# Turning a kernel's intermediate outputs by DMA transposes on ScalarE's queue, with a new order of the first loads

## The chip, the cores and the metric

The kernel runs on one core of one Trainium2 chip. The metric is the device time of one execution in microseconds; several executions are run and their median is given. A profile of one further execution shows what each engine did.

The engines are named as in the profile: PE is TensorE (matmuls; its weight loads are PEld), DVE is VectorE, ACT is ScalarE, POOL is GpSimd, SP is SyncE, which here only issues loads. ACTq and SPq are the instruction queues of ACT and SP, which issue transfers.

## The reference

```python
def _attn_ref(q, k, v, alpha):                     # each (4, 8, 768, 48), float32
    B, H, S, D = q.shape
    state = np.zeros((B, H, D, D), dtype=np.float32)
    y = np.zeros_like(q)
    for t in range(S):
        state = alpha[:, :, t, :, None] * state + np.einsum('bhd,bhe->bhde', k[:, :, t], v[:, :, t])
        y[:, :, t] = np.einsum('bhd,bhde->bhe', q[:, :, t], state)
    return y

def _moe_ref(x, w1, w2, w3, w_out):                # x (3072, 384), w1..w3 (384, 768), w_out (768, 384)
    h = np.maximum(np.maximum(x @ w1, x @ w2), x @ w3)
    return h @ w_out
```

The output y of the gated recurrence, heads side by side, is the input x of the feed-forward part. alpha lies between 0.8 and 1.0.

## The kernel before

**Tiling.** Time is cut into six chunks of 128 steps. A unit is one chunk of one batch with all eight heads: 24 units, u = 0 to 23, four per chunk. Two units are a group, n = 0 to 11. Group n's inputs q, k, v and alpha are loaded together (384 KB each, in rows of 192 bytes) into one of five sets of buffers (`ld[x][n % 5]`).

**A unit.** `decay` takes the logarithm of alpha for a group (L482, ACT) and its totals (L495, PE). `prep(u)` sums the logarithms along time by a matmul with a triangular matrix (L523), takes two exponentials (L526, L528, ACT), multiplies them onto q and k (L535, POOL or DVE as the table `EARLY` says), scales v (L546 on POOL, or L541 on ACT), turns q and k on PE (L556) and copies them out (L560, DVE), forms the scores (L568, PE) and masks them (L574, DVE). `output(u)` multiplies the masked scores with v (L594) and, after the first chunk, q with the carried state Z (L591); ACT scales the result into the fp16 tile `xb` (L602); PE turns `xb` in three 128 x 128 squares (L609, the step `turn`), and DVE copies the turned squares into `xT` (L613). `state(u)` carries the state on (L627 PE, L633 DVE, L640 POOL, or DVE in the first chunk).

**The feed-forward stage**, `ffn(n)`, works on a group's 256 tokens. The maximum of three products is taken as x w1 + max(0, x (w2 - w1), x (w3 - w1)), so `wd` holds the two differences, made by the four `subs` (L430, DVE), and w1 is multiplied with w_out beforehand (`turned`, L447 and L453; `folded`, L464 and L471). A stage is 36 matmuls with wd (L665), six ReLU on ACT (L675) and maxima on DVE (L680), 18 matmuls with w1o and wo (L696), two copies on ACT (L706) and two stores issued from ACT's queue (L707).

**Order.** Nothing is scheduled at run time: each engine executes its instructions in the order of the program. `Plan` collects all steps with an engine, a planned cost and a rank; `order` simulates the engines, the PSUM banks, the transfers and the clock of PE with these figures, lets every engine take the step that can start first (the lower rank where several can), and emits the instructions in the order of the planned start times. Ranks: unit u has rank u, stage n starts at 2n + `LEAD`. The order of the loads on SP is the list `FIRST` for groups 0 to 3 and the weights, and then group by group. The weights are loaded in pieces of columns, cut at `WCUTS` (rows for w_out), cast on ACT where needed (L422), and w1's and w_out's fp32 copies share one buffer.

Of the kernel before, what the change touches and what calls it, by code (L numbers as in the profile page):

```python
# [10 lines left out]
FP32 = mybir.dt.float32  # L11
# [16 lines left out]
DMA_OUT = {"SP": 0.9, "POOL": 0.9}  # L28
DMA_BOTH = {"SP": 0.2, "POOL": 0.85}
SPARE = 1.5  # L30
LEAD = 7.0
EARLY = {0: ("DVE", "POOL", "POOL"), 1: ("POOL", "DVE", "POOL"), 2: ("POOL", "DVE", "POOL"),
         3: ("POOL", "DVE", "ACT"), 4: ("POOL", "DVE", "POOL"), 5: ("POOL", "DVE", "POOL"),
         6: ("DVE", "DVE", "POOL"), 8: ("POOL", "POOL", "ACT")}
WEIGHTS = ()
WCUTS = (0, 256, 768)
SUBS = {(1, 0): "DVE", (1, 1): "DVE", (2, 0): "DVE", (2, 1): "DVE"}
FIRST = (("a", 0, 1, 2), ("k", 1, 0, 1), ("aq", 0, 0, 1), ("qk", 0, 1, 2), ("k", 0, 0, 1),
# [5 lines left out]
CLOCK_WINDOW, CLOCK_PHASE, CLOCK_WAKE, CLOCK_KEEP = 3.413, 0.0, 0.75, 0.37  # L44


# [65 lines left out]
class Plan:  # L112
# [10 lines left out]
        self.behind, self.tail = {}, {}  # L123

    def step(self, eng, cost, rank, run, reads=(), writes=(), banks=(), load=0.0, line=None,
             mode=0, late=0.0):
        i = len(self.steps)
        deps = set()
        if line is not None:
            if line in self.tail:  # L130
                self.behind[i] = self.tail[line]
            self.tail[line] = i
        for k in reads:
            if k in self.writer:
                deps.add(self.writer[k])
        for k in writes:
            if k in self.writer:
                deps.add(self.writer[k])
            deps.update(self.readers.get(k, ()))
        for k in reads:  # L140
            self.readers.setdefault(k, []).append(i)
        for k in writes:
            self.writer[k] = i
            self.readers[k] = []
        deps.discard(i)
        for k in set(reads) | set(writes):
            if k in self.users:
                self.users[k].append(i)
        for k in banks:
            self.users[k] = [i]  # L150
        self.steps.append((eng, cost, rank, run, deps, tuple(banks), load, mode, late))

    def homes(self, bank_free, keys):
        left, when, at = dict(bank_free), 0.0, {}
# [13 lines left out]
    def order(self):  # L168
# [41 lines left out]
        while len(seq) < n:  # L210
            best = None
            for e, cand in pending.items():
                pick = None
                for i in cand:
                    at = self.homes(bank_free, self.steps[i][5])
                    if at is None:
                        continue
                    t = max(ready[i], free[e], at[0])
                    turn = TURN_RANK if e == "PE" and self.steps[i][7] != mode else 0.0
                    key = (t, self.steps[i][2] + turn, i)  # L220
                    if pick is None or key < pick:
                        pick = key
                if pick is not None and (best is None or pick < best[0]):
                    best = (pick, e)
            landing = dma.next()
            if landing and (best is None or landing[0] <= best[0][0]):
                end, i = dma.next(commit=True)
                self.landed[i] = end
                finish(i, end)
                continue  # L230
            (t, _, i), e = best
            _, cost, _, _, _, banks, load, m, late = self.steps[i]
            pending[e].discard(i)
            for k, b in self.homes(bank_free, banks)[1].items():
                place[k] = b
                for j in range(self.width.get(k, 1)):
                    del bank_free[b + j]
            if e == "PE":
                if m != mode:
                    mode = m  # L240
                    cost += TURN_COST
                cost = clock.run(t, cost)
            free[e] = t + cost
            seq.append((t, i))
            if load:
                dma.add(e, t + cost + DMA_IN[e], load, i, late)
            else:
                finish(i, t + cost + HOP[e])
            if i in follows:
                arrive(follows[i], t)  # L250
        self.times = {i: t for t, i in seq}
# [4 lines left out]
def kernel(  # L256
# [69 lines left out]
    v16s = homes(7, [P, H, D], FP16, "v")  # L326
    qkTs = homes(3, [P, 2, NP, P], FP16, "qkT")
    LAs = homes(3, [P, 2, NP, P], FP16, "LA")
    xbs = homes(3, [P, DM], FP16, "xb")
    xTs = homes(NX, [P, NFT, TG], FP16, "xT")  # L330
    hTs = homes(3, [P, NJ, TG], FP16, "hT")
    obs = homes(4, [P, DM], FP32, "ob")
# [18 lines left out]
        for t in zz:  # L351
            nc.vector.memset(t, 0.0)

    plan = Plan({x: range(NBANKS) for x in ("Lp", "hp", "tp", "A", "yp", "xp", "pp", "gp", "op", "wt", "wp")})
    place = {}

    psall = pspool.tile([P, NBANKS, 512], FP32, name="psum")
# [20 lines left out]
    def load(n, lo, hi, names="aqkv"):  # L378
        cb, g = divmod(n, B // UB)
        for x in names:  # L380
            t = ld[x][n % 5]

            def run(x=x, t=t):
                nc.sync.dma_start(  # L384
                    t[:, lo:hi],
                    views[x][cb * P:(cb + 1) * P, g * HG + lo:g * HG + hi])

            plan.step("SP", 0.5, -1.0, run, line="loads",
                      writes=[(x, n % 5, h) for h in range(lo // H, hi // H)],
                      load=(1.84 if n < 3 else 1.96) * (hi - lo) / HG,  # L390
                      late=0.0 if n < 3 else SPARE)

    nparts = len(WCUTS) - 1
# [18 lines left out]
    def wload(g, part):  # L412
# [1 line left out]
                  lambda: nc.sync.dma_start(  # L414
                      piece(wst[g], g, part),
                      piece(matrices[g].rearrange("(t p) f -> p t f", p=P), g, part)),
                  writes=[("ws", g % 3, part)], line="loads",
                  load=3.1 * (WCUTS[part + 1] - WCUTS[part]) / DF)
        if g in (0, 3):
            n = NFT * (WCUTS[part + 1] - WCUTS[part])  # L420
            plan.step("ACT", 0.2 + 0.00083 * n, -0.5,
                      lambda: nc.scalar.copy(out=piece((w1h, 0, 0, wo16)[g], g, part),  # L422
                                             in_=piece(wst[g], g, part)),
                      reads=[("ws", g % 3, part)], writes=[("w", g, part)])

    def subs(g, part):
        cols = slice(WCUTS[part], WCUTS[part + 1])
        n, eng = NFT * (cols.stop - cols.start), SUBS[g, part]
        plan.step(eng, 0.2 + n * (0.0023 if eng == "POOL" else 0.00106), 0.0 if g == 1 else 3.0,
                  lambda: (nc.gpsimd if eng == "POOL" else nc.vector).tensor_sub(  # L430
                      wd[:, :, g - 1, cols], wst[g][:, :, cols], w1h[:, :, cols]),
                  reads=[("ws", g, part), ("w", 0, part)], writes=[("wd", g, part)])
# [79 lines left out]
    def prep(u):  # L512
# [47 lines left out]
        plan.step("DVE", 0.69, u, lambda: nc.vector.tensor_copy(out=qkT, in_=live[tk]),  # L560
                  reads=[tk], writes=[("qkT", u % 3)])

        def scores():
            live[Ak] = banks2(Ak, FP32)
            for j in range(NP):
                for p in range(2):
# [1 line left out]
                    nc.tensor.matmul(live[Ak][:, p, j * P:(j + 1) * P],  # L568
                                     qkT[rows, 1, j, :], qkT[rows, 0, j, :], start=True, stop=True)

        plan.step("PE", 0.23, u, scores, banks=[Ak], mode=1,
                  reads=[("qkT", u % 3), ("qkT room", u % 3)], writes=[Ak, ("LA room", u % 3)])
        plan.step("DVE", 1.3, u,
                  lambda: nc.vector.tensor_mul(  # L574
                      LA.rearrange("p a b t -> p (a b) t"),
                      live[Ak].rearrange("p a (b t) -> p (a b) t", t=P),
                      maskA.unsqueeze(1).broadcast_to([P, H, P])),
                  reads=[Ak], writes=[("LA", u % 3)])

    def output(u):  # L580
        n, i = divmod(u, UB)
        cb, b = divmod(u, B)
        qkT, LA, v16, xb = qkTs[u % 3], LAs[u % 3], v16s[u % 7], xbs[u % 3]
        Z = Zs[cb % 2][b]
        yk, xk = ("yp", u), ("xp", u)

        def outs():
            yp = live[yk] = bank(yk, [P, H, D], FP32)
            for j in range(NP):
# [3 lines left out]
                for p in range(2):  # L593
# [4 lines left out]
                  reads=[("qkT", u % 3), ("LA", u % 3), ("v16", u % 7), ("qkT room", u % 3),  # L598
                         ("LA room", u % 3)]
                  + ([("Z", cb % 2, b)] if cb else []))  # L600
        plan.step("ACT", 0.58, u,
                  lambda: nc.scalar.activation(out=xb, in_=live[yk].rearrange("p a b -> p (a b)"),  # L602
                                               func=AFT.Copy, scale=ysc),
                  reads=[yk], writes=[("xb", u % 3)])

        def turn():
            live[xk] = bank(xk, [P, NFT, P], FP16)
            for ft in range(NFT):
                nc.tensor.transpose(live[xk][:, ft, :], xb[:, ft * P:(ft + 1) * P], ident)  # L609

        plan.step("PE", 0.17, u, turn, banks=[xk], reads=[("xb", u % 3)], writes=[xk])
        plan.step("DVE", 0.35, u,
                  lambda: nc.vector.tensor_copy(out=xTs[n % NX][:, :, i * P:(i + 1) * P], in_=live[xk]),  # L613
                  reads=[xk], writes=[("xT", n % NX, i)])

    def state(u):
        n, i = divmod(u, UB)
# [102 lines left out]
    for n in range(NG):  # L720
# [5 lines left out]
                state(u)  # L726
        for u in range(n * UB, (n + 1) * UB):
            prep(u)
            for g, after, x in WEIGHTS:
                if after == u:  # L730
                    weights(g, ("v16", u % 7) if x == "v" else ("qk", u % 7, "qk".index(x)))
            output(u)
        for key in SUBS:
            if not made[key] and ("w", 0, 0) in plan.writer and ("ws", *key) in plan.writer:
                made[key] = True
# [40 lines left out]
```

## Time and profile before

| | before |
|---|---|
| median of 3 runs (us) | 159.06 (157.92 to 159.46) |
| profiled execution (us) | 158.94 |
| its span, first to last instruction (us) | 157.2 |
| PE busy (us, share of the span) | 137.1 (87%) |
| DVE / ACT / POOL busy (us) | 102.3 / 86.3 / 68.6 |
| read from HBM / written (MB) | 23.69 / 4.72 |
| L609 PE / L613 DVE (turns of xb) | 72 instructions / 24 instructions |

Times are in microseconds. A group of instructions is a line of the kernel with an engine and an operation; behind its busy time and the mean of one in nanoseconds stands the idle time of the engine just before these instructions, with what ended it. Several matmuls can be in flight at once, so that the records of single ones overlap. In the chain of work that ended last, each piece of time belongs to one engine only. A loading transfer shows twice: its issue on SPq, which is long when the queue is full, and its landing.

### The profile page before, as it was taken

What the parts mean: (1) busy time and instruction counts of PE and PEld (TensorE: products, weight loads), DVE (VectorE), ACT (ScalarE), POOL (GpSimd) and SP (SyncE); (2) the same over time, 40 slices, a digit from 0 to 9 for tenths busy, and PEclk for the clock granted to TensorE, in tenths of its full rate; (3) what the DMA queues carried; (4) which work ended last, traced back from release to release, by engine and by line L of the source; (5) the groups of instructions that cost most, each with busy time, mean ns of one, the idle gap of its engine ahead of it and who ended that gap; (6) DMA issues with size and microseconds to landing.
All of it is one profiled execution on the core that took longest, in us unless ns stands there. A gap on an engine that the chain in (4) does not pass through costs nothing.

```text
span 157.2 us, 4036 instructions
## 1 busy us (share of the span) xinstructions
PE 137.1 (87%) x1612; PEld 105.2 (67%) x1612; DVE 102.3 (65%) x172; ACT 86.3 (55%) x172; POOL 68.6 (44%) x98
## 2 busy tenths in 40 slices
PE   0264479599999999999899998999999999999990
PEld 0142357467687796888678777688797787868650
DVE  7058573588985997979759987357698494224020
ACT  3607476877176775785548546369356335424321
POOL 0051242005206285979969886279939500000000
PEclk9999999999999999999999999999999999999999
DMA  5999999989999999999999999999920110202112
GB/s 118 217 281 237 352 205 356 305 181 225 208 216 233 221 220 201 269 205 216 190 207 275 173 255 223 233 261 197 230 76 0 54 50 0 104 8 92 50 50 100
DMA packets 106226, 28.66 MB, mean 182 GB/s; under 512 B 99936, under 2 KB 105056, under 8 KB 106208
## 3 DMA queue, kind: packets, MB, share of 16 engines
q1 hardware_dynamic: 102464, 23.60, 71.9%
q10 hardware_dynamic: 3744, 4.82, 8.6%
q8 instruction: 12, 0.20, 0.5%
q14 instruction: 6, 0.05, 0.1%
HBM read 23.69 MB, written 4.72 MB: 181 GB/s over the span
## 4 chain that ended last, share of the span: by engine, by line
PE 58%; SPq 28%; DMA 7%; issue 2%; ACT 2%; POOL 1%; ACTq 0%
PE psum L665 23%; SPq L384 23%; PE psum L696 17%; DMA an<-in_alpha_dram 7%; SPq L414 5%; PE psum L556 4%; PE psum L568 3%; PE psum L523 2%; PE psum L609 2%; PE psum L594 2%; PE psum L591 2%; PE psum L627 2%; PE psum L495 1%; POOL qk L535 1%; ACT ob L706 1%
## 5 line engine op out<-in xcount | busy, mean ns | idle before, releaser
L665 PE MATMUL psum<-xT,wd 128*128 128x256 f16 x432 | 55.4, 276 | 1.7 <-DVE wd L430 1.6
L665 PEld LDWEIGHTS <-wd 128*128 128x128 f16 x432 | 40.8, 99 | 8.6 <-DVE wd L430 2.1
L680 DVE TENSOR_TENSOR hT<-psum,hT 128x512 f16<-128x512 f32 x36 | 24.4, 688 | 18.2 <-PE psum L665 14.4
L535 POOL TENSOR_TENSOR qk<-qn,ep 128x384 f16<-128x384 f32 x22 | 22.3, 1017 | 30.2 <-ACT ep L526 20.1
L574 DVE TENSOR_TENSOR LA<-psum,c 128x1024 f16<-128x1024 f32 x24 | 28.8, 1218 | 2.8 <-PE psum L568 2.7
L675 ACT ACTIVATE hT<-psum 128x512 f16<-128x512 f32 x36 | 21.3, 598 | 15.7 <-PE psum L665 14.9
L696 PE MATMUL psum<-wo,hT 128*128 128x384 f16 x144 | 27.3, 326 | 0.0
L706 ACT COPY ob<-psum 128x384 f32<-128x384 f32 x24 | 11.5, 480 | 19.7 <-PE psum L696 18.6
L546 POOL TENSOR_SCALAR v<-vn,c 128x384 f16<-128x384 f32 x22 | 13.5, 618 | 18.4 <-DMA vn<-in_v_dram 18.3
L556 PE MATMUL psum<-c,qk 128*128 128x128 f16 x192 | 16.5, 231 | 4.5 <-POOL qk L535 4.4
L696 PEld LDWEIGHTS <-hT 128*128 128x128 f16 x144 | 14.1, 98 | 9.3
L535 POOL TENSOR_TENSOR qk<-kn,en 128x384 f16<-128x384 f32 x18 | 18.0, 1000 | 2.6 <-DMA kn<-in_k_dram 1.5
L560 DVE COPY qkT<-psum 128x1024 f16<-128x1024 f16 x24 | 16.3, 687 | 3.7 <-PE psum L556 3.4
L640 POOL TENSOR_TENSOR Z<-U,G 48x192 f16<-48x192 f32 x32 | 15.7, 503 | 5.6 <-DVE U L633 4.5
L556 PEld LDWEIGHTS <-qk 128*128 128x128 f16 x192 | 12.5, 102 | 6.5 <-POOL qk L535 5.8
L482 ACT ACTIVATE la<-an 128x768 f16<-128x768 f32 (+1 forms) x15 | 10.7, 714 | 11.0 <-DMA an<-in_alpha_dram 11.0
L602 ACT ACTIVATE xb<-psum,c 128x384 f16<-128x384 f32 x24 | 13.9, 579 | 3.4 <-PE psum L594 1.9
L696 PE MATMUL psum<-w1o,xT 128*128 128x384 f16 x72 | 15.6, 326 | 0.0
L526 ACT ACTIVATE ep<-psum 128x384 f32<-128x384 f32 x24 | 11.8, 491 | 5.5 <-PE psum L523 2.5
L613 DVE COPY xT<-psum 128x384 f16<-128x384 f16 x24 | 8.5, 355 | 8.2 <-PE psum L609 7.9
L523 PE MATMUL psum<-la,c 128*128 128x384 f16 x24 | 8.5, 353 | 6.1 <-ACT la L482 6.0
L594 PE MATMUL psum<-v,LA 128*128 128x48 f16 x192 | 11.4, 187 | 0.9 <-POOL v L546 0.8
(38 smaller groups left out, 148.2 us busy)
## 6 DMA issues: line engine op xcount, KB each, us to landing
out_dram<-ob ACTq DMA_DIRECT2D x24, 192.0 KB, 2.9
an<-in_alpha_dram SPq DMA_DIRECT2D x9, 384.0 KB, 5.9
qn<-in_q_dram SPq DMA_DIRECT2D x9, 384.0 KB, 6.4
kn<-in_k_dram SPq DMA_DIRECT2D x9, 384.0 KB, 6.1
vn<-in_v_dram SPq DMA_DIRECT2D x9, 384.0 KB, 6.2
ws<-in_moe_w_dram SPq DMA_DIRECT2D x3, 768.0 KB, 6.6
an<-in_alpha_dram SPq DMA_DIRECT2D x6, 192.0 KB, 4.1
kn<-in_k_dram SPq DMA_DIRECT2D x6, 192.0 KB, 4.4
```

What stands on the lines that cost most here:

```text
L384: nc.sync.dma_start(t[:, lo:hi], views[x][cb * P:(cb + 1) * P, g * HG + lo:g * HG + hi])
L535: nc.gpsimd if eng == "POOL" else nc.vector).tensor_mul(
L556: nc.tensor.transpose(live[tk][:, w, j, :], qk[:, w, 2 * j:2 * j + 2, :], ident)
L560: plan.step("DVE", 0.69, u, lambda: nc.vector.tensor_copy(out=qkT, in_=live[tk]), reads=[tk], writes=[("qkT", u % 3)])
L574: lambda: nc.vector.tensor_mul(LA.rearrange("p a b t -> p (a b) t"), live[Ak].rearrange("p a (b t) -> p (a b) t", t=P), maskA.unsqueeze(1) ...
L594: nc.tensor.matmul(yp[:, 2 * j + p, :], LA[:, p, j, :], v16[:, 2 * j + p, :], start=(cb == 0), stop=True, skip_group_check=True)
L602: lambda: nc.scalar.activation(out=xb, in_=live[yk].rearrange("p a b -> p (a b)"), func=AFT.Copy, scale=ysc),
L640: eng.tensor_mul(Zn[rows, :, cols], U[rows, :, cols], G[rows, i * NP:(i + 1) * NP].unsqueeze(2).broadcast_to([D, NP, D]))
L665: nc.tensor.matmul(live[gk][:, jj, :], wd[:, kt, g, c0:c0 + P], xT[:, kt, :], start=(kt == 0), stop=(kt == NFT - 1))
L675: lambda h=h, gk=gk: nc.scalar.activation(out=h, in_=live[gk], func=AFT.Relu),
L680: lambda h=h, gk=gk: nc.vector.tensor_max(h, live[gk], h),
L696: nc.tensor.matmul(live[ok], a[:, i * P:(i + 1) * P], w, start=(kt == 0), stop=(kt == nk - 1))
```

## The change

- **Turns.** From unit 8 on (`CROSS = 8`), `output` no longer has the steps `turn` (PE) and the copy to `xT` (DVE). Its new step `across` on ACT scales the result into `xb` and then issues a transposing transfer from ACT's queue that writes `xb` turned into `xT`. The plan counts 0.93 us for it, with another 3.5 (`TURNED`) until `xT` can be read. `xb` has five buffers instead of three. The planned cost of a load of group 4 and later rises by `PAUSE`, 0.3 us.
- **Order of the loads.** `FIRST` begins with q, alpha, k and v of group 0, and then has pieces of w2, w1 and w3, then group 1 and w_out between them. The weights are cut in three pieces instead of two (`WCUTS`), which gives twelve loads instead of eight and six subtractions instead of four. w_out's loads now wait for all the casts of w1, whose buffer they use.
- **Engines.** Five of the six subtractions are on POOL, and `EARLY` gives other engines to products and scalings of the first ten units.
- **Dummy matmuls.** `warm(1, 0, 60)` adds 60 matmuls of zeros (128 x 256, result unused) behind unit 1's product of q, at rank 90, so where the plan has nothing else for PE.
- **Figures of the plan.** `LEAD` is 5 instead of 7, and some planned costs are other ones. `PAIRS = 99` leaves the order of the scores as it was.

```diff
-LEAD = 7.0
-EARLY = {0: ("DVE", "POOL", "POOL"), 1: ("POOL", "DVE", "POOL"), 2: ("POOL", "DVE", "POOL"),
-         3: ("POOL", "DVE", "ACT"), 4: ("POOL", "DVE", "POOL"), 5: ("POOL", "DVE", "POOL"),
-         6: ("DVE", "DVE", "POOL"), 8: ("POOL", "POOL", "ACT")}
+LEAD = 5.0
+EARLY = {0: ("DVE", "DVE", "ACT"), 2: ("POOL", "DVE", "ACT"), 3: ("POOL", "POOL", "ACT"),
+         4: ("POOL", "POOL", "ACT"), 5: ("DVE", "POOL", "POOL"), 6: ("POOL", "POOL", "POOL"),
+         7: ("DVE", "DVE", "ACT"), 8: ("POOL", "POOL", "POOL"), 9: ("POOL", "DVE", "POOL")}
-WCUTS = (0, 256, 768)
-SUBS = {(1, 0): "DVE", (1, 1): "DVE", (2, 0): "DVE", (2, 1): "DVE"}
-FIRST = (("a", 0, 1, 2), ("k", 1, 0, 1), ("aq", 0, 0, 1), ("qk", 0, 1, 2), ("k", 0, 0, 1),
-         ("w", 1, 0), ("w", 0, 0), ("a", 1, 0, 1), ("q", 1, 0, 1), ("v", 1, 0, 1), ("w", 0, 1),
-         ("w", 1, 1), ("v", 0, 1, 2), ("v", 0, 0, 1), ("k", 1, 1, 2), ("a", 1, 1, 2),
-         ("q", 1, 1, 2), ("w", 3, 1), ("w", 2, 0), ("w", 3, 0), ("v", 1, 1, 2), ("w", 2, 1),
-         ("aqkv", 2, 0, 2), ("q", 3, 0, 1), ("a", 3, 0, 1), ("k", 3, 0, 1), ("a", 3, 1, 2),
+WCUTS = (0, 256, 512, 768)
+SUBS = {(1, 0): "POOL", (1, 1): "POOL", (1, 2): "POOL", (2, 0): "POOL", (2, 1): "DVE",
+        (2, 2): "POOL"}
+FIRST = (("q", 0, 0, 1), ("a", 0, 0, 1), ("q", 0, 1, 2), ("a", 0, 1, 2), ("k", 0, 0, 1),
+         ("v", 0, 0, 1), ("w", 1, 1), ("kv", 0, 1, 2), ("w", 1, 0), ("w", 0, 0), ("w", 2, 0),
+         ("w", 0, 2), ("w", 0, 1), ("w", 2, 1), ("w", 1, 2), ("q", 1, 0, 1), ("ak", 1, 0, 1),
+         ("akq", 1, 1, 2), ("w", 3, 1), ("w", 2, 2), ("v", 1, 0, 1), ("w", 3, 0), ("w", 3, 2),
+         ("v", 1, 1, 2), ("aqkv", 2, 0, 2), ("a", 3, 0, 1), ("qk", 3, 0, 1), ("a", 3, 1, 2),
          ("k", 3, 1, 2), ("v", 3, 0, 1), ("q", 3, 1, 2), ("v", 3, 1, 2))
+WARM = (1, 0, 60)
+PAIRS, CROSS = 99, 8
+TURNED, PAUSE = 3.5, 0.3
...
-    xbs = homes(3, [P, DM], FP16, "xb")
+    xbs = homes(5, [P, DM], FP16, "xb")
...
-                      load=(1.84 if n < 3 else 1.96) * (hi - lo) / HG,
+                      load=(1.84 if n < 3 else 2.02 if n < CROSS // 2 else 2.02 + PAUSE) * (hi - lo) / HG,
...
-                  writes=[("ws", g % 3, part)], line="loads",
-                  load=3.1 * (WCUTS[part + 1] - WCUTS[part]) / DF)
+                  reads=[("ws room", p) for p in casting[0]] if g == 3 else [],
+                  writes=[("ws", g, part)], line="loads",
+                  load=3.2 * (WCUTS[part + 1] - WCUTS[part]) / DF)
...
+        if u >= CROSS:
+            def across():
+                nc.scalar.activation(out=xb, in_=live[yk].rearrange("p a b -> p (a b)"),
+                                     func=AFT.Copy, scale=ysc)
+                nc.scalar.dma_start_transpose(out=xTs[n % NX][:, :, i * P:(i + 1) * P], in_=xb)
+
+            plan.step("ACT", 0.93, u, across, reads=[yk], after=TURNED,
+                      writes=[("xb", u % 5), ("xT", n % NX, i)])
+            return
...
+    def warm(u, w, count):
+        live["wm"] = None
+
+        def zeros():
+            live["wm"] = bank(("wm", 0), [P, TG], FP32)
+            nc.tensor.matmul(live["wm"], Zs[1][0].rearrange("p a b -> p (a b)")[:, :P],
+                             Zs[1][0].rearrange("p a b -> p (a b)")[:, :TG], start=True, stop=True)
+
+        for i in range(count):
+            plan.step("PE", 0.11, 90.0, zeros, banks=[("wm", 0)] if i == 0 else [], line="warm",
+                      reads=[("qk", u % 7, w)] if i == 0 else [],
+                      writes=[("wm", 0)] if i in (0, count - 1) else [])
...
+            if u == WARM[0]:
+                warm(*WARM)
```

More of the change, by code (lines that the diff above doesn't have):

```diff
@@ L125, in step @@
     def step(self, eng, cost, rank, run, reads=(), writes=(), banks=(), load=0.0, line=None,
-             mode=0, late=0.0):
+             mode=0, late=0.0, after=0.0):
         i = len(self.steps)
@@ L150, in step @@
             self.users[k] = [i]
-        self.steps.append((eng, cost, rank, run, deps, tuple(banks), load, mode, late))
+        self.steps.append((eng, cost, rank, run, deps, tuple(banks), load, mode, late, after))
     def homes(self, bank_free, keys):
@@ L231, in order @@
             (t, _, i), e = best
-            _, cost, _, _, _, banks, load, m, late = self.steps[i]
+            _, cost, _, _, _, banks, load, m, late, after_ = self.steps[i]
             pending[e].discard(i)
@@ L247, in order @@
             else:
-                finish(i, t + cost + HOP[e])
+                finish(i, t + cost + HOP[e] + after_)
             if i in follows:
@@ L352 @@
             nc.vector.memset(t, 0.0)
-    plan = Plan({x: range(NBANKS) for x in ("Lp", "hp", "tp", "A", "yp", "xp", "pp", "gp", "op", "wt", "wp")})
+    plan = Plan({x: range(NBANKS) for x in ("Lp", "hp", "tp", "A", "yp", "xp", "pp", "gp", "op", "wt", "wp", "wm")})
     place = {}
@@ L423, in wload @@
                                              in_=piece(wst[g], g, part)),
-                      reads=[("ws", g % 3, part)], writes=[("w", g, part)])
+                      reads=[("ws", g, part)],
+                      writes=[("w", g, part)] + [("ws room", part)] * (g == 0))
     def subs(g, part):
@@ L428, in subs @@
         n, eng = NFT * (cols.stop - cols.start), SUBS[g, part]
-        plan.step(eng, 0.2 + n * (0.0023 if eng == "POOL" else 0.00106), 0.0 if g == 1 else 3.0,
+        plan.step(eng, 0.2 + n * (0.0019 if eng == "POOL" else 0.00102), 0.0 if g == 1 else 3.0,
                   lambda: (nc.gpsimd if eng == "POOL" else nc.vector).tensor_sub(
@@ L561, in prep, with scores @@
                   reads=[tk], writes=[("qkT", u % 3)])
-        def scores():
+        def scores(u=u, Ak=Ak, qkT=qkT):
             live[Ak] = banks2(Ak, FP32)
@@ L569, in scores, with product, both @@
                                      qkT[rows, 1, j, :], qkT[rows, 0, j, :], start=True, stop=True)
[L571 to L578, printed above, removed]
+        def product(u=u, Ak=Ak, qkT=qkT, LA=LA):
+            plan.step("DVE", 1.22, u,
+                      lambda: nc.vector.tensor_mul(
+                          LA.rearrange("p a b t -> p (a b) t"),
+                          live[Ak].rearrange("p a (b t) -> p (a b) t", t=P),
+                          maskA.unsqueeze(1).broadcast_to([P, H, P])),
+                      reads=[Ak], writes=[("LA", u % 3)])
+        if u < PAIRS:
+            plan.step("PE", 0.23, u, scores, banks=[Ak], mode=1,
+                      reads=[("qkT", u % 3), ("qkT room", u % 3)], writes=[Ak, ("LA room", u % 3)])
+            product()
+        elif i == 0:
+            held.append((scores, product, u, Ak))
+        else:
+            first, made, v, Bk = held.pop()
+            def both():
+                first()
+                scores()
+            plan.step("PE", 0.46, v, both, banks=[Bk, Ak], mode=1,
+                      reads=[("qkT", x % 3) for x in (v, u)] + [("qkT room", x % 3) for x in (v, u)],
+                      writes=[Bk, Ak] + [("LA room", x % 3) for x in (v, u)])
+            made()
+            product()
+    held = []
     def output(u):
@@ L582, in output @@
         cb, b = divmod(u, B)
-        qkT, LA, v16, xb = qkTs[u % 3], LAs[u % 3], v16s[u % 7], xbs[u % 3]
+        qkT, LA, v16, xb = qkTs[u % 3], LAs[u % 3], v16s[u % 7], xbs[u % 5]
         Z = Zs[cb % 2][b]
@@ L603, in output @@
                                                func=AFT.Copy, scale=ysc),
-                  reads=[yk], writes=[("xb", u % 3)])
+                  reads=[yk], writes=[("xb", u % 5)])
         def turn():
@@ L609, in turn @@
                 nc.tensor.transpose(live[xk][:, ft, :], xb[:, ft * P:(ft + 1) * P], ident)
-        plan.step("PE", 0.17, u, turn, banks=[xk], reads=[("xb", u % 3)], writes=[xk])
+        plan.step("PE", 0.17, u, turn, banks=[xk], reads=[("xb", u % 5)], writes=[xk])
         plan.step("DVE", 0.35, u,
@@ L728 @@
             prep(u)
+            if u >= PAIRS and u % UB == 0:
+                continue
+            if u == WARM[0]:
+                warm(*WARM)
             for g, after, x in WEIGHTS:
@@ L731 @@
                     weights(g, ("v16", u % 7) if x == "v" else ("qk", u % 7, "qk".index(x)))
-            output(u)
+            for v in (u - 1, u) if u >= PAIRS else (u,):
+                output(v)
         for key in SUBS:
```

## The prediction

> **What bounds the kernel now.** I read the stage table first, then the queue table, the chain of work that ended last, and the groups by line. The stage table (columns: length, then busy time and instructions of TensorE's matmuls, its weight loads, VectorE, ScalarE, GpSimd; then granted clock, DMA share, GB/s) splits the span in three:
>
> ```profile
> 0.00:34.60 34.60, 19.72 (x188) 13.34 (x188) 20.34 (x39) 19.46 (x33) 6.63 (x11) 1.00 1.01 250
> 34.60:115.50 80.90, 79.69 (x1051) 62.79 (x1052) 63.32 (x105) 49.69 (x107) 55.41 (x78) 1.00 1.07 222
> 115.50:152.90 37.40, 37.40 (x379) 29.03 (x375) 18.62 (x30) 16.27 (x33) 6.58 (x10) 1.00 0.12 43
> ```
>
> Until 34.6 us TensorE waits for loads. After that it is idle for 1.2 us in 118.3: it is the bound, from 34.6 to 152.9. The DMA engines are full until 115.5 (share 1.07), then nearly empty, so the loads are not the bound, but they stop 37.4 us before TensorE does. That distance is the cover for everything that slows them. The queue table gives what they carry (packets, MB, share of 16 engines):
>
> ```profile
> q1 hardware_dynamic: 102464, 23.60, 71.9%
> q10 hardware_dynamic: 3744, 4.82, 8.6%
> ```
>
> q1 is SP's loads, q10 ScalarE's 24 stores. The chain, in order of time, gives the true price of each TensorE step (its records of single matmuls overlap):
>
> ```profile
> 88.95 0.17 PE psum L609 x3
> 89.12 0.34 PE psum L627 x8
> 89.46 0.45 PE psum L556 x8
> 89.91 1.46 PE psum L696 x9
> 134.56 3.93 PE psum L665 x36
> 148.27 1.96 PE psum L665 x18
> 152.87 0.49 ACT ob L706
> ```
>
> With 0.33 for eight L568, 0.16 for one L523, 0.18 for eight L495 (the same chain) and 0.37 for the 16 of L591 and L594 (timeline at 94 us), a group of two units costs TensorE 0.32 + 0.18 + 0.90 + 0.66 + 0.74 + 0.34 + 0.68 = 3.82 us, and its feed-forward stage 3.93 + 2.92 = 6.85: 10.67. All work is then 12 x 6.85 + 10 x 3.82 + 2 x 2.8 (the first chunk, without Z) + 3.95 (w1's turns and the folding) = 130.0 us. Counted by line, 12.2 us of it lay before 34.6; 117.8 remain, and the trace used 118.3. The bookkeeping closes, so I forecast with it.
>
> **Part 1, the turns leave TensorE.** The groups touched:
>
> ```profile
> L602 ACT ACTIVATE xb<-psum,c 128x384 f16<-128x384 f32 x24 | 13.9, 579 | 3.4 <-PE psum L594 1.9
> L613 DVE COPY xT<-psum 128x384 f16<-128x384 f16 x24 | 8.5, 355 | 8.2 <-PE psum L609 7.9
> L706 ACT COPY ob<-psum 128x384 f32<-128x384 f32 x24 | 11.5, 480 | 19.7 <-PE psum L696 18.6
> out_dram<-ob ACTq DMA_DIRECT2D x24, 192.0 KB, 2.9
> ```
>
> Units 8 to 23 lose `turn`: 16 x 0.17 = **-2.7 us**, all after 34.6, where TensorE has no slack, so in full. VectorE loses 16 x 0.355 = 5.7 us; it was not the bound (63 of 81 us), so I count nothing.
>
> **Part 2, what the transposing transfers cost.** The trace has none, so three prices are bounded.
> Issue on ScalarE: a store's issue takes 0.34 us there (L707), a load's on SP's full queue 1.35 to 1.60 (L384 medians). I take 0.34, as ScalarE's own queue has never shown more than 0.40. ScalarE's work per group is then 0.85 (Ln) + 0.28 + 4 x 0.49 + 2 x 0.58 + 3 x 0.60 + 2 x 0.48 = 7.0, plus four issues, 1.4: 8.4 of TensorE's 10.33. Queued behind each issue are the next Exp, the ReLU that frees a PSUM bank and the copy of a finished output, on which VectorE and TensorE wait. I charge **+0.6 us** in all for such meetings.
> Landing: stores land in 1.9 to 4.4 us, loads in 3.3 to 8.1; I take 4. Matmul, ScalarE copy, turn and VectorE copy took about 1 us. Nothing waits for the extra 3 us, because xT is read late: the last L609 ended at 133.1, and of the 54 L665 after 141.41 the last group's stage has 36, so it began no earlier than 143.4, a cover of 10 us. Without cover each of 16 units would cost 3 us.
> Time taken from the loads, p per unit: 96 KB at the stores' rate is 0.086 x 157.2 / 4.82 MB, or 0.28 us; in packets of 192 B like the loads' (17.7 ns of one engine each, 512 of them over 16) 0.56; in packets of one element, 49,152, it would be 54 us. I take 0.56, as rows of xb are contiguous like the loads'. The last load (issued at 109.39, its tensor first read at 115.6) then lands 14 x 0.56 = 7.8 us later, at 123.4. A group of loads takes 8.2 + 1.1 = 9.3 us, still less than TensorE's 10.33, so the backlog keeps growing and the cost on the path is nothing; the cover is gone at p = 1.1 for the pace, and at p = 1.6 for the end (rival D).
> The Trainium skill has two rules here that disagree. "Advanced Engine Details and Errata" (X-Bar Transpose (TRN2)) says a transposing transfer is as fast as a plain one; by it p is near 0.28 and the sum stays. "VectorE: DVE Perf Modes" (The three transpose paths) gives 1309 ns for a 128x128 square by DMA against 390 by TensorE; three squares would make 3.9 us, as a landing time harmless, as engine time an estimate far beyond the cover. No row of this case decides between them.
>
> **Part 3, the start.** Bytes to the first four matrices and two groups stay at 7.9 MB, so all of it lands near 31 us as now. What changes is what TensorE can do meanwhile. Now v of group 0 is issued only at 13 us and w3's last piece at 23.7, so `outs` begins at 21.8 and the first L665 at 24.5, after which it waits for wd. In the new order group 0's 1.57 MB are in at about 9 us (1.8 MB had moved by 10), unit 0's turn ends near 14 (7 for k, then 0.6 + 0.9 + 0.7 + 1.4 + 0.7 + 2.0 for product, turns, copy, scores and mask, outputs, xb and xT), and most of w1, w2, w3 near 20. So by 30 us TensorE can have done group 0 (2.8), w1's turns (1.0), the L665 of stage 0 (3.9) and most of group 1's own part (2.4): 10.1, and from there it has work queued (folding 2.95, L665 of stage 1) without a gap: 14.5 at 34.6, against 12.2 now. I take **-1.7 us** of these 2.3; the bounds are +2 (a late piece stalls the in-order queue) and -4 (never idle from 24 us on).
> Edits inside this part: the subtractions go mostly to GpSimd, 768 elements at L535's 2.65 ns, 2.0 us each instead of VectorE's 0.96, five times 10 us in a stretch where GpSimd was busy 6.6 of 34.6; each is 1.1 us later, inside the bound. Weights in three pieces instead of two add four issues on SP (0.5 each; SP's queue is fuller than it can send anyway) and 0.4 us of casts. The 60 dummy matmuls are placed after unit 1's q product at the lowest rank; at 0.11 us (L665) 6.6 us, twice that in the slow start (eight L568 take 0.61 us at 11 us and 0.33 later, at a granted clock of 1.00 both times). TensorE's idle time there, 14.9 us, holds them; if they clump before real work they cost up to 6.6. I take 0. LEAD 5 puts feed-forward stages earlier against units; both are TensorE work and the sum is unchanged: 0, between -1 and +1.
>
> **Sum.** The profiled execution took 158.94 us: span 157.2 and 1.74 around it; the tail after the last matmul is 4.3 us and stays. 158.94 - 2.7 + 0.6 - 1.7 = 155.1, rounded to **155.0 us**. The profiled run lies 0.1 under the median of the runs shown (159.06), so it needs no correction: 2.5% faster.
>
> **Rivals.**
> A, the forecast: TensorE stays the bound and loses the turns. Chance 0.55, own range 152.5 to 157.3.
> B, the newly planned order meets a chip that runs otherwise, and gaps eat the gain: -2.7, no gain at the start, and 2 to 3 us more of stalls (one waiting instruction holds all of TensorE; the order before had only 1.2 us). 158.5. Against it: ScalarE, VectorE and GpSimd all have room. Chance 0.15.
> C, ScalarE becomes the pace: an issue there takes what SP's takes, 1.6 us. Per group 7.0 + 0.7 + 3.2 = 10.9 against 10.33, 0.6 x 8 groups = 4.6, and about as much for the bunching, less in the tail: 155 + 7 = 162. It decides from 1.3 us per issue. For it: SP's issues do stretch; against: 24 ScalarE issues never did beside the same loads. Chance 0.12.
> D, the transposing transfers hold the engines and the loads become the bound. After the last v has landed at 115.3 + 14p come at least v's scaling, outputs and xb (1.6), the landing (4), the stage (6.85), copy and store (3.4): 16, so the time is 133 + 14p. It passes the forecast at p = 1.6 and the time before at 1.85; at 2.05, the spacing of a whole load now (63.5 us for 31), it is 162. For it: the queues are full; against: 96 KB is a quarter of a load. The slower rule of the VectorE page named above belongs here. Chance 0.16, with 0.02 more for element-wise packets (hundreds of us).
>
> **How the numbers follow.** A measurement can tell about 1% from no change. Faster by over 1% is A and the lucky end of B: 0.57; within 1%, the rest of B: 0.13; slower, C and D: 0.30. The range reaches from A's low end, 152.5, to a little beyond C and D's prices, 164, leaving out D with larger p and the far bound.
>
> **What would show it.** Right: L609 x24 instead of x72, L613 x8; TensorE idle under 2 us from 34 us to its end, that end near 149; last load read near 123; first L665 near 16 to 18 us; transposes issued in about 0.4 us and landed in 3 to 5. Wrong: loads spaced more than 2.6 us apart in the second half and waits of L523, L482 or L546 on loads (D); ScalarE issues over 1 us with L675 or L706 late (C); L665 waiting for xT's transfer; gaps before L665 or L464 in the first 35 us (B).

## The result and the profile after

The changed kernel takes 164.89 us (163.47 to 165.12) against 159.26 for the kernel before: the ratio is 1.035 (1.029 to 1.041), slower by 5.6 us where 155.0 was forecast. The profiled execution took 164.81 us, span 162.9. The mean granted clock of these executions was 0.99, in the one of 163.47 it was 1.00; in the profiled one it fell between 32 and 38 us (below).

The stage table of the changed kernel, cut at the same first border, at the first use of its last load, and at TensorE's end (columns as in the prediction):

```profile
0.00:34.60 34.60, 22.42 (x234) 17.04 (x235) 17.76 (x36) 18.36 (x33) 14.55 (x15) 0.98 0.99 242
34.60:126.50 91.90, 86.80 (x1074) 66.42 (x1073) 59.69 (x95) 54.15 (x116) 53.79 (x75) 0.99 1.17 210
126.50:158.50 32.00, 30.87 (x319) 23.73 (x318) 15.52 (x22) 13.93 (x28) 7.81 (x12) 1.00 0.24 68
```

TensorE is idle for 6.2 us after 34.6, not 1.2, and ends at 158.5, not 152.9. The turns did leave it, and the transposing transfers stand in ScalarE's queue. Groups by line, and ScalarE's queue instructions and landings of xT (the first line is of the list of groups, the second of the tile's list, in ns, the third its landing time):

```profile
L644 PE MATMUL psum<-c,xb 128*128 128x128 f16 x24 | 2.8, 241 | 1.0 <-ACT xb L637 1.0
L631 ACTq DMA_TRANSPOSE xT<-xb x16: 1194/1204/1757, 65.9 to 144.8; - x16
DMA to landing us min/median/max: 2.3/4.6/7.2
```

24 matmuls instead of 72, and 16 issues of at least 1.19 us each (minimum, median, maximum); the prediction took 0.34. What such a pair does is seen in ScalarE's timeline (start, length, engine, instruction; in brackets the idle time before it and what ended it):

```profile
76.57 0.58 ACT L629 ACTIVATE xb<-psum,c 128x384 f16<-128x384 f32 x1
77.18 1.70 ACTq L631 DMA_TRANSPOSE xT<-xb  x1
78.93 0.27 ACT L507 ACTIVATE e<-psum,c 128x16 f32<-128x16 f32 x1 [1.78 <-issue]
79.11 0.48 ACT L532 ACTIVATE ep<-psum 128x384 f32<-128x384 f32 x1
79.48 0.58 ACT L629 ACTIVATE xb<-psum,c 128x384 f16<-128x384 f32 x1
80.09 1.20 ACTq L631 DMA_TRANSPOSE xT<-xb  x1
81.33 0.49 ACT L534 ACTIVATE en<-psum 128x384 f32<-128x384 f32 x1 [1.27 <-POOL qk L541]
```

The issue waits for xb, then nothing of ScalarE runs until it is done. Behind the second one stands the second exponential of a unit, 81.33, which frees a PSUM bank. (Its bracket names a product on POOL, but that one ended at 80.67, and the issue at 81.29.) TensorE's own waits of 45 to 152 us name it (what waited, for what: us, times, longest):

```profile
PE psum L744 <- ACT en L534: 2.8, 3, 1.4
PE psum L562 <- POOL qk L541: 2.1, 4, 0.6
PE psum L675 <- ACT e L507: 0.8, 1, 0.8
PE psum L675 <- ACT en L534: 0.4, 1, 0.4
```

POOL's products, the second line, in turn wait for the exponentials. (The sum of such waits proves little: POOL's q product waits 43.6 us for `ep` here and 20.5 before, but also 40.1 in e9 below, where TensorE hardly stops.) The pieces of the chain in order of time show the same pair on the path:

```profile
87.35 0.59 ACT xb L629
87.96 1.20 ACTq L631
89.16 0.05 issue
89.21 0.06 ACT e L507
89.27 0.07 issue
89.38 0.48 ACT ep L532
89.86 0.48 ACT xb L629
90.37 1.20 ACTq L631
91.56 0.05 issue
91.61 0.50 ACT en L534
```

From 87.35 to 92.11 the chain is ScalarE's, and 2.4 us of it are two issues.

### The profile page after: what moved, and what is told of

It is laid out like the page before. It is cut to its first block, busy times and chain, and to the rows that moved or that the text cites. A ratio compares the mean times of both kernels' runs of the same rounds, so it can differ in the third digit from the quotient of the medians.

```text
span 162.9 us, 4069 instructions
## 1 busy us (share of the span) xinstructions
PE 140.4 (86%) x1624; PEld 107.2 (66%) x1624; DVE 93.0 (57%) x152; ACT 87.4 (54%) x177; POOL 76.1 (47%) x101
## 3 DMA queue, kind: packets, MB, share of 16 engines
q10 hardware_dynamic: 10400, 6.40, 15.5%
## 4 chain that ended last, share of the span: by engine, by line
PE 56%; ACT 10%; ACTq 9%; DMA 8%; SPq 8%; POOL 3%; issue 3%; DVE 1%; DVEq 0%
PE psum L713 23%; PE psum L744 15%; ACTq L631 9%; DMA ws<-in_moe_w_dram 5%; PE psum L562 4%; PE psum L574 4%; SPq L418 4%; SPq L388 4%; DMA ws<-in_moe_w_out_dram 4%; ACT xb L629 3%; POOL qk L541 3%; PE psum L470 2%; ACT en L534 2%; PE psum L529 2%; ACT ep L532 2%
## 5 line engine op out<-in xcount | busy, mean ns | idle before, releaser
L713 PE MATMUL psum<-xT,wd 128*128 128x256 f16 x432 | 56.0, 273 | 1.1 <-DVE xT L648 1.0
L541 POOL TENSOR_TENSOR qk<-qn,ep 128x384 f16<-128x384 f32 x21 | 21.4, 1019 | 52.0 <-ACT ep L532 43.6
L713 PEld LDWEIGHTS <-wd 128*128 128x128 f16 x432 | 39.7, 98 | 7.8 <-issue 1.2
L541 POOL TENSOR_TENSOR qk<-kn,en 128x384 f16<-128x384 f32 x20 | 20.3, 1017 | 5.4 <-ACT en L534 5.0
L532 ACT ACTIVATE ep<-psum 128x384 f32<-128x384 f32 x24 | 11.7, 488 | 4.5 <-PE psum L529 4.5
L534 ACT ACTIVATE en<-psum 128x384 f32<-128x384 f32 x24 | 11.8, 491 | 4.2 <-POOL qk L541 3.0
L629 ACT ACTIVATE xb<-psum,c 128x384 f16<-128x384 f32 x16 | 9.4, 585 | 7.5 <-DVE hT L728 3.1
L620 PEld LDWEIGHTS <-LA 128*128 128x128 f16 x192 | 10.1, 99 | 2.3 <-issue 1.1
(42 smaller groups left out, 157.2 us busy)
```

Source lines behind the costliest of these rows:

```text
L532: plan.step("ACT", 0.49, u, lambda: nc.scalar.activation(out=ep, in_=live[Lk], func=AFT.Exp), reads=[Lk], writes=[("ep", u % 3)])
L534: plan.step("ACT", 0.49, u, lambda: nc.scalar.activation(out=en, in_=live[Lk], func=AFT.Exp, scale=-1.0), reads=[Lk], writes=[("en", u % 3)])
L541: nc.gpsimd if eng == "POOL" else nc.vector).tensor_mul(
L620: nc.tensor.matmul(yp[:, 2 * j + p, :], LA[:, p, j, :], v16[:, 2 * j + p, :], start=(cb == 0), stop=True, skip_group_check=True)
L713: nc.tensor.matmul(live[gk][:, jj, :], wd[:, kt, g, c0:c0 + P], xT[:, kt, :], start=(kt == 0), stop=(kt == NFT - 1))
```

## The experiments

The theories: 1, the length of the issue on ScalarE; 2, the transfers themselves (landing, bytes, late loads); 3, the start and `LEAD`; 4, loads that wait for ScalarE's transfers through completion counters. The last comes from SP's waits in the changed kernel. In the kernel before, no load waited for a transfer:

```profile
SPq L388 <- DMA xT<-xb: 7.5, 4, 4.1
SPq L388 <- DMA out_dram<-ob: 5.7, 4, 4.0
```

In the trace the transfers take eight completion counters in turn, in the order of the program, and each waits for the one that had its counter before. So a load waits for the transfer eight places ahead, also where that is a late one of ScalarE's; the last load is issued at 120.4 instead of 109.4. To compare amounts of work, I price each matmul record by its line as in the prediction and add up what was begun by a certain time ("priced work"; the dummies count nothing).

**No transposes.** `CROSS = 8` becomes 99.

> The changed kernel with CROSS at 99: all 24 units turn on TensorE again, everything else (order of the first loads, pieces, dummies, LEAD 5) stays. Theory 1 (each transposing issue holds ScalarE's queue for 1.2 us, and what is queued behind it makes TensorE wait; the start costs about 2.6 us by itself): the 16 turns come back (+2.7), the stalls from 45 us on go (about -5), so about 162.5. Theory 2 (the transposes take DMA time and the late loads are the cost): the loads end again near 115 us and the time is about the same as in theory 1; the two are told apart by the run with ScalarE held. Theory 3 (the start and LEAD 5 are the whole loss): 164.9 + 2.7, about 167.

159.33 us, 1.000 (0.996 to 1.004): not the 162.5 of theory 1's sum, and far from theory 3's 167. The new start with its order costs and brings nothing, and the loss of 5.6 us goes with the transposes. Part of the difference between the two profiles is older than they are, though: by 45 us, ahead of the first such transfer at 65.9, the changed kernel had begun 19.8 us of priced work and e1 22.2, with the same order until 50 us, but with a clock that fell in the one and stayed at 1.00 in the other.

**The turns alone**, put into the kernel before.

> The kernel before with the transposing transfers from unit 8 on as its only change (with TURNED, PAUSE and five xb), the old start and LEAD 7. Theory 1: 159.3 - 2.7 + about 5 of stalls = 161.5. Theory 3 (only the start loses): 159.3 - 2.7 = 156.6.

161.38 us, 1.013 (1.007 to 1.019), as theory 1 had it. In the old order the same 16 issues cost 2.1 us net; theory 3 is out.

**ScalarE held without transfers.** In e1's kernel, from unit 8 on, planned as 0.93 us:

```diff
+            if u >= HOLD:
+                nc.scalar.copy(out=idle, in_=wst[1].rearrange("p t f -> p (t f)")[:, :1200])
```

> As e1_no_transposes, but from unit 8 on ScalarE does a copy of 1200 elements of 128 partitions (about 1.2 us, result unused) behind each xb, planned as 0.93 us for both, as the plan has it for the transposes: it holds ScalarE as long as a transposing issue does, with no transfer. Theory 1: about 5 us over e1_no_transposes, some 167.5, with TensorE's idle time between 60 and 145 us near the 6 us of the changed kernel. Theory 2 (the transfers themselves cost): within 1 us of e1_no_transposes.

161.1 us, 1.009 (1.005 to 1.014): 1.8 over e1 and not 5. But this copy overlaps its neighbours: from the start of xb to ScalarE's next instruction it took 1.57 us on average, in the changed kernel 2.02.

**The issue in the plan.** `plan.step("ACT", 0.93, u, across, ...)` becomes 1.85.

> The changed kernel with one number different: the plan counts 1.85 us for the scaling and the issue instead of 0.93, so that the order is made for the issue as it is. If the stalls come from an order that does not know the issue's length: most of the 5 us come back, 160 to 161. If ScalarE simply has too little room (10.1 us of work a group against TensorE's 10.3): 163.5 to 165.

160.69 us, 1.008 (1.003 to 1.013). The same instructions in another order give back 4.2 of the 5.6 us, as was expected if the order were at fault; against ScalarE's having too little room (163.5 to 165) this run speaks clearly. Now TensorE also waits for a landing:

```profile
PE psum L713 <- DMA xT<-xb: 2.4, 2, 1.8
```

**The hold as long as it is.** The copy of e3 with 1750 elements, same order:

> As e3_act_held with a copy of 1750 elements instead of 1200: in the changed kernel the step from the start of xb to the next instruction of ScalarE is 2.02 us on average (issues of 1.20 to 1.76), in e3_act_held it was 1.56, so that run held ScalarE for too short a time. Theory 1 (the hold is the cause): the stalls grow faster than the hold, 164 or more (e1_no_transposes 159.3). Theory 2 (the transfers, with their landing and their share of the DMA engines, are the cause): 161.5 to 162, the step of e3_act_held scaled by 1.55 / 1.08.

164.7 us, 1.040 (1.031 to 1.049); ScalarE's step is 2.01 us. Another 0.44 us a unit, 7.0 in all, cost 3.6 us, some of it by the clock (0.94 from 80 to 100 us in this profile, 1.00 in e3's). The effect is there without any transposing transfer.

**Hold and a small transfer.** In e3's kernel, behind the copy:

```diff
+                nc.scalar.dma_start(away[u % 5], xb[:, :64])
```

> As e3_act_held with a plain transfer of 16 KB (xb's first 64 columns to a tile that nothing reads) issued from ScalarE behind each copy, which brings ScalarE's step to about 2.0 us too, and puts 16 more transfers among the loads in the program's eight completion counters (each transfer takes over the counter of the one eight places ahead in the program and waits for it), with hardly any bytes. Theory 4 (loads wait for late transfers of ScalarE through the counters): loads end some 5 us later than in e5_hold_matched and the time is over it by 1 to 3. Without such an effect: equal to e5_hold_matched within 0.7.

162.13 us, 1.012 (1.003 to 1.021). This one missed its aim: the issue stands behind the copy and ran while the copy was still running, so that the step stayed at 1.57 and the run compares with e3 (161.1). In its profile no load waits for one of the small transfers, and the last load is issued at 108.6, as in e3; theory 4 got no support. Late loads were not without effect here: an alpha that landed at 93.5, 91.4 in e3, held ScalarE's queue, and TensorE waited 1.7 us for the xb behind it.

**Issue and landing in the plan**: 2.0 on ScalarE, `TURNED` 5.5.

> The changed kernel with the plan's numbers set to what the trace shows: 2.0 us on ScalarE and 5.5 us until xT can be read (it lands 4.6 after its issue, up to 7.2; e4_issue_planned still waited 2.4 us for it). If order is all that is wrong: 2 us under e4_issue_planned, 158.7. If the room on ScalarE and in the DMA queues is what lacks: 160 to 161, as there.

169.72 us, 1.069 (1.064 to 1.075). Both expectations failed. With figures near the measured ones the order came out 9 us worse than e4's, though ScalarE's step is no longer (1.95 against 2.03). TensorE is idle for 9.0 us from 45 to 145 us, 3.9 in e4, in many waits of different kinds; the longest, 2.2 us at 86, is for VectorE's maximum. The granted clock was lower too: 0.64 from 30 to 34.6 us and 0.91 from 80 to 100, in e4 1.00 in both. Why the plan does worse with better figures stays open.

**Issued from SP.** `nc.sync.dma_start_transpose` in a step of its own on SP.

> The changed kernel with the transposes issued from SP's queue instead of ScalarE's (planned as 1.2 us there): the same transfers with ScalarE free. Theory 1: the stalls behind ScalarE go, 160 to 161, unless the loads behind the transposes in SP's queue wait too long. Theory 2: about as the changed kernel, 164 to 165, with the loads ending near 125 us or later.

186.32 us, 1.173 (1.168 to 1.179). It tells nothing on theory 1: loads have rank -1 in the plan and went ahead of the transposes, twelve of which follow the last load:

```profile
112.28 1.03 SPq L388 DMA_DIRECT2D vn<-in_v_dram  x1
113.40 53.98 SPq L633 DMA_TRANSPOSE xT<-xb  x12
```

TensorE waited 28.5 us for xT at 71.4.

**A plain transfer in place of the transposing one**, everything else in place:

```diff
-                nc.scalar.dma_start_transpose(out=xTs[n % NX][:, :, i * P:(i + 1) * P], in_=xb)
+                nc.scalar.dma_start(xTs[n % NX][:, :, i * P:(i + 1) * P],
+                                    xb.rearrange("p (f t) -> p f t", f=NFT))
```

> The changed kernel, same order of instructions on every engine, with one thing replaced: ScalarE issues a plain transfer of the same 96 KB from xb to the same place in xT instead of a transposing one, so the squares stay unturned (this part of the computation is left out). The wait for its landing stays, the bytes stay; the issue takes 0.34 us as a store's does instead of 1.20 to 1.76. Theory 1 (the length of the issue on ScalarE): the stalls of 6 us between 60 and 145 us mostly go, 158.5 to 160. Theory 2 (landing, bytes on the DMA engines, late loads, or the order itself): 163 to 165.

156.67 us, 0.980 (0.973 to 0.987): 8.2 us under the changed kernel, more than theory 1 had expected. The issue takes 0.60 us and the step 1.32; bytes and landing are about the same:

```profile
L631 ACTq DMA_DIRECT2D xT<-xb x16: 602/607/687, 64.9 to 135.8; - x16
DMA to landing us min/median/max: 2.1/4.1/5.4
```

**The same and held.** Behind the plain transfer a copy of 1050 elements on ScalarE.

> As e9_plain_transfer, with a copy of 1050 elements on ScalarE behind each plain transfer (result unused), which brings the step from xb to ScalarE's next instruction back to the 2.02 us of the changed kernel. Theory 1: 164 to 165.5, the changed kernel's time, with no transposing transfer in it. Theory 2: within 1 us of e9_plain_transfer.

165.11 us, 1.037 (1.032 to 1.043): the changed kernel's time with no transposing transfer in it (the step was 2.24, 0.22 longer than there, because the plain issue takes 0.60 here and not 0.34; a small cost of the transposing transfer itself is therefore not excluded). The stages from 45 to 145 us of before, the changed kernel, e9 and e10, in this order:

```profile
45.00:145.00 100.00, 98.82 (x1258) 78.44 (x1255) 70.93 (x118) 58.55 (x122) 58.50 (x83) 1.00 0.79 169
```

```profile
45.00:145.00 100.00, 93.76 (x1193) 73.27 (x1192) 67.87 (x102) 56.14 (x118) 57.73 (x82) 1.00 1.01 183
```

```profile
45.00:145.00 100.00, 99.43 (x1245) 78.35 (x1242) 68.86 (x104) 60.13 (x125) 57.82 (x82) 1.00 0.87 184
```

```profile
45.00:145.00 100.00, 92.29 (x1180) 72.12 (x1178) 66.43 (x102) 69.84 (x132) 57.73 (x82) 1.00 0.85 180
```

TensorE's idle time is 1.2, 6.2, 0.6 and 7.7 us. It goes with the hold, not with the transfer; and its waits in e10 name the same instructions as in the changed kernel:

```profile
PE psum L747 <- ACT en L535: 3.8, 3, 1.7
PE psum L563 <- POOL qk L542: 2.3, 4, 0.6
```

**The last four units alone**, in the kernel before, planned as 1.85.

> The kernel before (old start, LEAD 7) with transposing transfers for units 20 to 23 alone, whose issues fall where the loads have ended and ScalarE is less than half busy, planned as 1.85 us. Theory 1: 4 x 0.17 us of TensorE saved and hardly a stall, 158.6 against 159.2, within the noise. If the transposes cost wherever they stand: 160 or more.

158.89 us, 0.999 (0.996 to 1.002), no difference that can be measured.

**No dummies**, in e1's kernel.

> e1_no_transposes without the 60 dummy matmuls: what they do to the start. If they keep TensorE's clock up: the first 34 us lose, 160 to 161 against 159.3. If they only fill idle time: equal, and the spread of the runs (158.1 to 161.7, with the granted clock at 0.99 in the slower ones) stays.

161.53 us, 1.012 (1.004 to 1.019): 2.2 over e1. The dummies, with the order that the plan makes for them (without them it differs from about 14 us on), are worth about 2 us. The trace is of the longest of the four executions, 163.38 us. In it TensorE stands idle for 3.05 us at 16.4 and has begun 19.7 us of priced work by 45, e1 22.2. Its matmuls also run slower: the first 12 L713 take 2.72 us at 22.4, in e1 24 of them take 2.78 at the same place, though the granted clock is shown as 1.00 in both.

No complete version was measured faster than the kernel before.

## Why the prediction was wrong

**The term that failed is the issue on ScalarE, part 2**: "I take 0.34". It is 1.20 in the median and 1.34 in the mean. The ends were both in the text, 0.34 and 1.60; the value was taken from the nearest queue, stores, and a transposing transfer is another instruction on it. Charged with +0.6 us, it cost some 7 to 8 in this order: the changed kernel lies 8.2 above e9 (164.89 against 156.67, with an issue of 0.60), and 0.9 of that had arisen in the two profiles by 45 us, before the first such transfer (19.8 against 20.7 us of priced work).

**Rival C was half right.** Its condition held: it decides from 1.3 us an issue, and the mean was 1.34. Its counter-argument, that 24 issues on this queue had never stretched, was an argument about stores. But that ScalarE becomes the pace the runs do not show. The 7.0 us of work a group add up records that overlap (0.48 long, but 0.37 from start to start, as at 79.11 in the timeline above). From 65 to 145 us ScalarE computed for 43.3 us, and issues took 21.5 for the transposes and about 5 for the stores: some 69 of 80, as the records overlap a little. In e4 it was occupied for as long, and e4 is 4.2 us faster. So there was room, and what cost time is the mechanism that part 2 itself named and charged with 0.6: an exponential, a ReLU or a copy that stands behind an issue comes late, and TensorE waits for it. That rival C's price, 162, is near 164.89 is in part luck.

**The turns** went as forecast. With the order of the changed kernel and a short issue, e9 is 2.3 us under the kernel before, near the 2.7 of part 1. With the start at zero and +0.6 for ScalarE the prediction's sum would be 156.8, and e9 took 156.67. That they agree so closely is partly luck: e9's profile was behind the kernel before at 45 us (20.7 against 22.2 us of priced work) and made up for most of it by 145 (95.7 against 94.5 in between).

**The start, part 3**, was mis-sized: -1.7 forecast, nothing measured (e1, 0.996 to 1.004). The priced work by 34.6 us is 12.1 in e1 and before, and 10.6 in the changed kernel's profile, not 14.5. Group 0 was early, but from 28 us on all that TensorE had left needed a late piece: w3's last part, v of group 1 and w_out, whose last two parts land at 32.2 and 33.4. The profile of the changed kernel:

```profile
29.82 1.64 POOL L436 TENSOR_TENSOR wd<-ws,w1h 128x768 f16<-128x768 f32 x1 [0.69 <-DMA ws<-in_moe_w_dram]
30.47 0.61 ACT L547 ACTIVATE v<-vn,c 128x384 f16<-128x384 f32 x1 [1.03 <-DMA vn<-in_v_dram]
31.14 0.36 PE L620 MATMUL psum<-v,LA 128*128 128x48 f16 x8 [1.55 <-ACT v L547]
32.26 0.83 ACT L427 CAST wo<-ws 128x768 f16<-128x768 f32 x1 [1.18 <-DMA ws<-in_moe_w_out_dram]
```

I had worked out when all bytes are in (31 us; the last v of group 1 landed at 34.3, in e1 at 32.9) but not which of them come last and what stands on those. The dummies, taken at 0, bring 2.2 of what the start has. And after TensorE's wait of 1.55 us the granted clock fell in the profiled execution, to 0.78, 0.50 and 0.87 in the stretches of 2 us from 32 to 38. The wait alone does not decide it: the kernel before waited 1.61 us until 29.9 and kept 1.00.

**Loads and landing (rival D)**: p was 0.56 and stayed harmless. q10's share rose from 8.6% of 157.2 us to 15.5% of 162.9, 11.7 us or 0.73 a transfer, stores that were slowed included (e9's plain transfers come to 0.51 by the same count). In e9 the loads end some 4 us later than before and it is the fastest run. Of the two rules weighed in the prediction, the Trainium skill's "Advanced Engine Details and Errata" (X-Bar Transpose (TRN2)) agrees with the landing: 4.6 us in the median against 4.1 for a plain transfer of the same bytes. The three squares, by the estimate 3.9 us, of the Trainium skill's "VectorE: DVE Perf Modes" (The three transpose paths) did not hold the engines (0.73). What decides here is the issue, of which the Trainium skill's "DMA: Bandwidth & Descriptors" (Issuing engines are not separate DMA queues) says that it is usually small relative to the transfer; with 1.20 against 4.6 us it is a quarter of it here, and ScalarE's own work waits for it.

**Order (rival B)** also matters, but not as forecast: e4 and e7 have the same instructions for the same issue and lie 9 us apart. The 7 to 8 us of the issue are those of this order, which was made for 0.93 us; e4's shows that another pays about 4 less.

## What to carry to other kernels

A transfer that replaces work on one engine is paid on another: before costing it at a store's price, ask how long its own kind of issue holds the queue, and what stands behind each issue that the bound engine will wait for. The issuing engine's average room does not answer that: with 69 of 80 us occupied, one order lost 5.6 us and another 1.4. Give the schedule the issue's length and measure what it makes of it: with 1.85 us planned the loss shrank to 1.4 us (e4), with 2.0 and a later landing it grew to 11 (e7). To tell an issue's length from the transfer's bytes and landing, put a plain transfer of the same bytes in the same place, and then add the hold back.

## What the runs showed of the hardware

- A transposing transfer of a 128 x 384 fp16 tile holds the issuing queue for 1.19 to 1.76 us on ScalarE (2.12 once in e4) and 1.18 to 3.28 on SP; a plain one of the same tile for 0.60, a store of 192 KB for 0.34. What stands behind the issue on ScalarE starts only after it. An issue behind a copy that it does not need ran beside that copy (a plain one, e6; no run has a transposing one there).
- The landing is not what it costs: 2.3 to 7.2 us beside full queues, 2.6 in the median from SP, mostly after the loads, and 2.3 to 2.4 in e11, after the loads.
- The loss grew faster than the hold: in one order, 1.57 us a step cost 1.8 us over e1 (which has an order of its own), 2.01 us cost 5.4.
- A stall of TensorE can cost more than its length, because the granted clock can fall after it: 1.55 us of waiting were followed by 0.78, 0.50 and 0.87 (changed kernel, 32 to 38 us), 1.61 us in the kernel before by 1.00.
